# Attention and two feed-forward layers in one kernel: row sums broadcast by two reads with 64 outermost rows, the store of x on SyncE's queue, a new fixed order

## The chip, the cores and the metric

The kernel runs on one core of one Trainium2 chip. The metric is the device time in microseconds (us) of one execution; less is better. The kernel before was timed in 3 runs: a median of 1224.97 us, from 1221.14 to 1226.95.

## The reference

Causal attention over 4 batches, 8 heads, 576 tokens and 64 values a head, mixed with a retrieval from a linear memory; its result x (2304 rows of 512) goes through two feed-forward layers of 512, 2048 and 512.

```python
scores = scale * q @ k.T                       # masked above the diagonal
a = exp(scores - scores.max(-1)); a /= a.sum(-1) + 1e-09
local = a @ v
q_p = phi(q)                                   # phi(x) = where(x > 0, x, exp(x) - 1) + 1
mem_out = (q_p @ M_prev) / (q_p @ z_prev + 1e-06)
g = sigmoid(beta)                              # one value for each head
x = g * mem_out + (1 - g) * local              # rows: tokens, columns: heads
h = x @ w_in;   x = where(h >= 1, h, where(h <= -1, 0, (h + 1) ** 2 / 4)) @ w_out
h = x @ w_in2;  x = maximum(0.01 * h, h) @ w_out2
```

## The kernel before

**Attention.** The work is cut into 16 units: 4 batches of 4 pairs of heads. `attention_unit(u)` writes down the tasks of one unit, each with an engine, a length in nanoseconds, a priority, the tasks that it needs, the buffers (`Room`) that it holds, and a due time after its end (`lag`). For one unit they are: k, q and v are loaded (`load_rows`, three DMAs each, on SyncE's queue); k and q are transposed by TensorE (k1, q1) and split into a high and a low part (k2, k3, q2, q3); GpSimd sets the last 64 rows of the two heads apart (`apart`, q4); phi(q) is formed (f1 to f3). The scores come in four parts s0 to s3 (`products`, L484 and L491); VectorE adds the mask and takes the row minimum of the negated scores (L506); ScalarE takes the exponential with its sum (L510). The exponentials are transposed in five groups (`turn`, TensorE at L419, ScalarE copies at L519) into `pa` and four `pb`. The product with v goes into the PSUM buffer O in three tasks: v0 (`values_a`, L534), v1 and v2 (`values_b`, L541 to L544).

**The row sums.** n1 computes the memory's norms into O (L550). l1 to l4 (VectorE, L555 to L560) turn the 9 columns of sums and 10 columns of norms into gate divided by sum, l5 (TensorE, L561) transposes the 19 columns into 19 rows of 128, l6 (ScalarE, L563) copies them to `rt`, l7 (SyncE, L564) writes them to the DRAM tensor `r_d[u]` of 19 rows in one DMA. l8 (SyncE, `spread`, L573) reads them back in three DMAs into R, a buffer of 128 partitions (64 for each of the two heads) by 2 planes by 576: plane 0 holds the factors of the softmax, columns 0 to 511 and 512 to 575 in a read each, plane 1 those of the memory. Each read has the source shape 2 x 64 x n, in which the 64 is a broadcast: every partition of a head gets the same row.

**The end of a unit.** m1 (TensorE, L582) forms the product with the memory in a W bank of PSUM. x1 (VectorE, `weigh`, L588, two steps) multiplies O by plane 0 of R, x2 (VectorE, L591) the W bank by plane 1, x3 (GpSimd, L593) adds the two planes, and a DMA issued by GpSimd (L594) stores the result in `x_d[b]`.

**The order.** `Plan.order()` makes one fixed order for each engine from the lengths, priorities (`10 * u + PRIO[key]`), needs, buffers and due times; `STAY` is a cost for TensorE to change its kind of matmul. No engine deviates from its order at run time. `ROOMS` says how many buffers of each kind there are: one O, three W, two R, two each of q, k and v. `EARLY` = 10 of the 16 half matrices of the first layer's weights are decoded by tasks of the same plan (`weight_half`), the others by the layers' own code. The 16 units, these tasks and the first two chunks of x for the first layer (`first_chunk`, after the four stores of batch 0) share the plan.

**The layers.** Behind the plan, `layer1_steps` and `layer2` go over chunks of 256 rows. They load x from `x_d`, split each operand into a high and a low part, and use three products for one. Their order is not touched by the change.

Of the kernel before, what the change touches and what calls it, by code (L numbers as in the profile page):

```python
# [8 lines left out]
F32 = mybir.dt.float32  # L9
# [8 lines left out]
B, H, S, D = 4, 8, 576, 64  # L18
NT, DM, DFF = B * S, H * D, 2048
NP = H // 2  # L20
# [18 lines left out]

PRIO = dict(load=-48.26, v=-40.11, mem=-30.82, k=-3.3, q=-1.74, phi=35.91, s0=-19.51, s1=-15.79, s2=6.04, s3=-14.57, ta=-66.58, tb0=-44.92,  # L40
            tb1=-21.43, tb2=-29.5, tb3=-16.11, v0=-23.74, n=-32.83, l=-36.92, v1=6.21, v2=23.96, m=23.51, x=55.42, w=(2.48, 4.3, 19.15), c=1.18)
EARLY, STAY = 10, 1.25
EVACUATE = dict(ta="ACT", tb0="ACT", tb1="ACT", tb2="ACT", tb3="ACT")
# [93 lines left out]
def attn_moe_moe_kernel(ctx, tc, q, k, v, m_prev, z_prev, beta, w1i, w1o, w2i, w2o, out):  # L137
    nc = tc.nc
# [10 lines left out]
    dram = ctx.enter_context(tc.tile_pool(name="dram", bufs=1, space=bass.MemoryType.DRAM))  # L149
# [75 lines left out]
    def at(room):  # L225
        return tiles[room.kind][room.slot]


    r_d = [dram.tile([19, 128], F32, name=f"r_d{u}") for u in range(B * NP)]
    x_d = [dram.tile([DM, S], F32, name=f"x_d{b}") for b in range(B)]  # L230
# [175 lines left out]
    act, vec, pe, pool = nc.scalar, nc.vector, nc.tensor, nc.gpsimd  # L406
# [16 lines left out]
    stored, memory_of = [], {}  # L423
    SEND = 570

    def attention_unit(u):
        b, p = UNITS[u]

        def add(engine, cost, key, after, rooms, fn, mode=None, lag=None):
            return plan.add(engine, cost, 10 * u + PRIO[key], after, rooms, fn, mode, lag)  # L430

        q, k, v = Room("q"), Room("k"), Room("v")
        ks, qs, ph, st, R, O = Room("ks"), Room("qs"), Room("ph"), Room("st"), Room("R"), Room("O")
# [8 lines left out]
        if p == 0:  # L442
            memory_of[b] = mem = Room("mem")
            memory_of[b] = mem, add("SP", 2 * SEND + 2 * SEND, "mem", (), [mem], load_mem)
        mem, ld_m = memory_of[b]
# [4 lines left out]
        t = Room("W")  # L450
# [6 lines left out]
        t = Room("W")  # L457
# [4 lines left out]
        q3 = add("DVE", dve(S), "q", [q2], [t, qs], lambda t=t: vec.scalar_tensor_tensor(  # L462
            out=at(qs)[:, 1, 0:S], in0=at(t)[:, 0:S], scalar=-0.125, in1=as_r(at(qs)[:, 0, 0:S]), op0=ALU.mult, op1=ALU.subtract))
# [6 lines left out]

        q4 = add("POOL", 600, "q", [q3], [qs], apart)
        f1 = add("ACT", from_psum(S), "phi", [q1], [t, ph], lambda t=t: act.activation(at(ph)[:, 0:S], at(t)[:, 0:S], AF.Exp))
# [90 lines left out]
        l6 = add("ACT", 180, "l", [l5], [O, rt], lambda: act.activation(at(rt)[0:19], at(O)[0:19, 384:512], AF.Copy))  # L563
        l7 = add("SP", 300, "l", [l6], [rt], lambda: nc.sync.dma_start(out=r_d[u], in_=at(rt)[0:19]), lag=2.4)  # L564

        def spread():
            flat = r_d[u].rearrange("r t -> (r t)")

            def rows(c0, step, n):
                return flat[c0:c0 + 2 * step].rearrange("(h t) -> h t", h=2)[:, 0:n].unsqueeze(1).broadcast_to([2, 64, n])  # L570

            for x, c0, c1, src in ((0, 0, 512, rows(0, 512, 512)), (0, 512, S, rows(1024, 64, 64)), (1, 0, S, rows(1152, 640, S))):
                nc.sync.dma_start(out=at(R)[:, x, c0:c1], in_=src)  # L573

        l8 = add("SP", 3 * SEND, "l", [l7], [R], spread, lag=2.5)
        v1 = add("PE", 1100, "v1", [tb[0], tb[1], ld_v], [pb[0], pb[1], v, O], lambda: values_b((0, 1)), "C")
# [9 lines left out]
        def weigh():  # L586
# [6 lines left out]
        x3 = add("POOL", 1450, "x", [x1, x2], [R], lambda: pool.tensor_tensor(at(R)[:, 0], at(R)[:, 0], at(R)[:, 1], ALU.add))  # L593
        stored.append(add("POOL", 1000, "x", [x3], [R], lambda: pool.dma_start(  # L594
            out=x_d[b][128 * p:128 * p + 128], in_=at(R)[:, 0])))
# [455 lines left out]
```

## Time and profile before

| what | value |
|---|---|
| median of 3 runs | 1224.97 us (1221.14 to 1226.95) |
| the profiled execution: its time | 1222.64 us |
| its span, first to last instruction | 1220.8 us |
| busy: TensorE, VectorE, ScalarE, GpSimd | 1072.3, 769.9, 515.2, 76.9 us |
| mean granted TensorE clock | 0.911 |
| moved by DMA | 110.94 MB, mean 91 GB/s |

The rows below come from one profiled execution. PE is TensorE's matmuls, PEld its weight loads, DVE VectorE, ACT ScalarE, POOL GpSimd, SP SyncE; a q behind a name (SPq) is what the engine's sequencer does, such as issuing a DMA. Times are us from the start of the span. "L573" is a line of the kernel. In a timeline row the brackets give the idle time of the engine ahead of the instruction and what ended it. The granted clock is a share of 2.4 GHz: 1.00 is the high level, 0.50 the low one (1.2 GHz). The DMA share is the mean busy share of 16 DMA engines; by its way of counting it can pass 1.

### The profile page before, as it was taken

How to read it: one execution, taken by the hardware profiler on the slowest of the kernel's cores; microseconds unless marked ns; L12 is line 12 of the kernel's file. 1: busy time of each engine (PE TensorE's matmuls, PEld its weight loads, DVE VectorE, ACT ScalarE, POOL GpSimd, SP SyncE). 2: the span in 40 equal slices, each digit the busy share in tenths (PEclk: the TensorE clock that was granted, in tenths of full speed). 3: DMA queues.
4: the chain of work that ended last, by engine and by line, in shares of the span. 5: the costliest groups of instructions: out<-in, count | busy, mean ns of one | idle time of the engine just before them, and what ended most of it. 6: DMA issues, size and time to landing. Idle time of an engine off the chain costs nothing.

```text
span 1220.8 us, 18534 instructions
## 1 busy us (share of the span) xinstructions
PE 1072.3 (88%) x7016; PEld 944.2 (77%) x7016; DVE 769.9 (63%) x1708; ACT 515.2 (42%) x988; POOL 76.9 (6%) x105
## 2 busy tenths in 40 slices
PE   6756667776766689999999999999999999999998
PEld 5544546555655467888898878899999999999997
DVE  5545556343433266648966766689888789775665
ACT  5534445443543034334453323345444445443432
POOL 1101011001101100000000000000000000121111
PEclk9767677776786699999999999999999999999999
DMA  5432442333211133224512542422332311122121
GB/s 125 124 89 85 110 133 64 85 110 85 73 53 45 40 113 95 83 91 138 156 53 79 163 133 92 138 70 87 121 104 94 98 53 53 53 77 80 54 86 52
DMA packets 124504, 110.94 MB, mean 91 GB/s; under 512 B 70224, under 2 KB 105600, under 8 KB 124416
## 3 DMA queue, kind: packets, MB, share of 16 engines
q1 hardware_dynamic: 121648, 104.49, 28.5%
q0 software_dynamic: 1280, 4.72, 1.0%
q8 instruction: 55, 0.90, 0.3%
q10 hardware_dynamic: 1488, 0.56, 0.2%
q14 instruction: 33, 0.27, 0.1%
HBM read 86.00 MB, written 23.75 MB: 90 GB/s over the span
## 4 chain that ended last, share of the span: by engine, by line
PE 67%; DMA 21%; DVE 7%; ACT 2%; issue 2%; SPq 1%; POOL 0%; DVEq 0%; ACTq 0%
DMA R<-r_d 19%; PE A L783 5%; PE A L782 5%; PE A L781 5%; PE A L711 5%; PE A L712 5%; PE A L710 5%; PE W L419 3%; PE y L806 3%; PE y L805 2%; PE y L804 2%; PE W L491 2%; PE y L740 2%; PE y L741 2%; PE y L742 2%
## 5 line engine op out<-in xcount | busy, mean ns | idle before, releaser
L783 PE MATMUL A<-ffn_x,i 128*128 128x256 f32 x576 | 163.1, 283 | 0.0
L781 PE MATMUL A<-ffn_x,i 128*128 128x256 f32 x576 | 163.0, 283 | 0.0
L782 PE MATMUL A<-ffn_x,i 128*128 128x256 f32 x576 | 163.0, 283 | 0.0
L720 ACT ACTIVATE g<-A 128x512 f32<-128x512 f32 (+1 forms) x80 | 44.3, 554 | 217.9 <-PE A L712 215.6
L419 PE MATMUL W<-ident,e 128*128 128x128 f32 x400 | 78.6, 353 | 65.5 <-DVE R L591 57.1
L419 PEld LDWEIGHTS W<-ident,e 128*128 128x128 f32 x400 | 62.0, 186 | 78.3 <-DVE R L591 60.0
L978 ACT ACTIVATE gh<-g 128x896 fp32r<-128x896 f32 x72 | 68.8, 955 | 124.8 <-PE A L805 72.4
L722 DVE SCALAR_TENSOR_TENSOR g<-A,g 128x512 f32<-128x512 f32 (+1 forms) x80 | 50.8, 635 | 96.5 <-ACT g L721 96.4
L783 PEld LDWEIGHTS A<-ffn_x,i 128*128 128x128 f32 x576 | 110.6, 192 | 0.0
L781 PEld LDWEIGHTS A<-ffn_x,i 128*128 128x128 f32 x576 | 110.6, 192 | 0.0
L782 PEld LDWEIGHTS A<-ffn_x,i 128*128 128x128 f32 x576 | 110.6, 192 | 0.0
L957 DVE TENSOR_TENSOR gl<-g,gh 128x896 fp32r<-128x896 f32 x72 | 86.6, 1203 | 33.4 <-ACT gh L978 33.4
L519 ACT ACTIVATE pb<-W 128x640 f32<-128x640 f32 x64 | 42.9, 675 | 147.2 <-PE W L419 147.0
L506 DVE CUSTOM_DVE_ANT_0 e<-W,mask 128x128 f32<-128x128 f32 (+3 forms) x144 | 67.7, 517 | 56.5 <-PE W L491 47.4
L510 ACT ACTIVATE e<-e,mx 128x128 f32<-128x128 f32 (+3 forms) x144 | 82.5, 574 | 18.7 <-DVE mx L506 18.5
L786 ACT ACTIVATE g<-A 128x512 f32<-128x512 f32 x72 | 42.8, 594 | 88.8 <-PE A L783 86.1
L829 POOL TENSOR_TENSOR ys<-ys,pp 128x512 f32<-128x512 f32 x16 | 27.1, 1718 | 751.3 <-DVE ys L824 751.3
L591 DVE TENSOR_TENSOR R<-W,R 128x576 f32<-128x576 f32 x16 | 12.1, 757 | 94.1 <-DMA R<-r_d 94.1
L710 PE MATMUL A<-ffn_x,i 128*128 128x512 f32 (+1 forms) x160 | 59.8, 374 | 11.1 <-DVE R L591 11.1
L534 PE MATMUL O<-pa,v 128*64 128x256 f32 (+1 forms) x128 | 20.3, 457 | 48.5 <-DVE R L588 48.2
L711 PE MATMUL A<-xl,i 128*128 128x512 f32 (+1 forms) x160 | 59.0, 369 | 0.6 <-DVE xl L683 0.6
L711 PE MATMUL A<-ffn_x,i 128*128 128x512 f32 (+1 forms) x160 | 59.4, 371 | 0.0
(212 smaller groups left out, 3034.0 us busy)
## 6 DMA issues: line engine op xcount, KB each, us to landing
raw<-in_moe_w_in_dram SPq DMA_DIRECT2D x32, 512.0 KB
raw<-in_moe_w_out_dram SPq DMA_DIRECT2D x32, 512.0 KB
xf<-y_d SPq DMA_DIRECT2D x18, 512.0 KB
xf<-x_d SPq DMA_DIRECT2D x10, 512.0 KB
R<-r_d SPq DMA_DIRECT2D x16, 288.0 KB
x_d<-R POOLq DMA_DIRECT2D x16, 288.0 KB, 2.4
xf<-yp_d SPq DMA_DIRECT2D x9, 512.0 KB
op_d<-ys SPq DMA_DIRECT2D x18, 256.0 KB
```

Of the source, the lines that this page charges most:

```text
L419: pe.transpose(t[:, c:c + 128], x, ident)
L506: lambda t=t, x=x, w=w, c=512 * h + c, mk=mk, col=col: vec.tensor_tensor_reduce(out=at(x)[:, 0:w], in0=at(t)[:, c:c + w], in1=mk, op0=ALU. ...
L510: lambda x=x, w=w, col=col: act.activation(at(x)[:, 0:w], at(x)[:, 0:w], AF.Exp, bias=at(st)[1][:, col:col + 1], scale=-1.0, accum_out=at( ...
L710: nc.tensor.matmul(hx, wh, xh[:, ct], start=(ct == 0), stop=False)
L711: nc.tensor.matmul(hx, wh, xl[:, ct], start=False, stop=False)
L712: nc.tensor.matmul(hx, wl, xh[:, ct], start=False, stop=(ct == 3))
L722: nc.vector.scalar_tensor_tensor(out=g, in0=hp, scalar=1.0, in1=g, op0=ALU.max, op1=ALU.min)
L781: nc.tensor.matmul(o, wh, xh[:, ct], start=(s == 0 and ct == 0), stop=False)
L782: nc.tensor.matmul(o, wh, xl[:, ct], start=False, stop=False)
L783: nc.tensor.matmul(o, wl, xh[:, ct], start=False, stop=(s == 1 and ct == 3))
L957: nc.vector.tensor_tensor(gl, g[:, 1:8], as_r(gh), ALU.subtract)
L978: nc.scalar.activation(gg[1], gg[0][:, 1:8], AF.Copy)
```

## The change

`r_d[u]` becomes a tensor of 2 heads x 2 planes x 640. `rows_out` (l7) writes it in three DMAs instead of one: the 8 rows of columns 0 to 511 of plane 0, the 10 rows of plane 1, and the row that holds columns 512 to 575 of plane 0 for both heads. `spread` (l8) reads it in two DMAs instead of three, one for each head: the destination is 64 partitions of R with both planes, the source shape is 64 x 2 x 576 with the broadcast outermost. The store of x is issued by SyncE instead of GpSimd, as a task of the plan. The lengths and due times in the plan are changed for four tasks: `apart` from 600 to 1150 ns, l7 from 300 to 900, l8 from 1710 to 1140 with the due time from 2.5 to 2.8 us, the store from 1000 on GpSimd to 570 on SyncE. All priorities and `STAY` have new values, so each engine's fixed order in the attention part is another one.

```diff
--- before.py
+++ after.py
@@ -37,9 +37,9 @@
 FETCH = {1: [24 + 4 * i for i in range(NW)] + [47 + 3 * i // 2 for i in range(16 - NW)]}
 HALVES = {N1: [82 + 7 * i // 2 for i in range(16)], N1 + 1: [x for x in range(150, 209) if x % 8 in (0, 6)]}
 
-PRIO = dict(load=-48.26, v=-40.11, mem=-30.82, k=-3.3, q=-1.74, phi=35.91, s0=-19.51, s1=-15.79, s2=6.04, s3=-14.57, ta=-66.58, tb0=-44.92,
-            tb1=-21.43, tb2=-29.5, tb3=-16.11, v0=-23.74, n=-32.83, l=-36.92, v1=6.21, v2=23.96, m=23.51, x=55.42, w=(2.48, 4.3, 19.15), c=1.18)
-EARLY, STAY = 10, 1.25
+PRIO = dict(load=-34.99, v=-34.71, mem=-17.36, k=6.9, q=2.05, phi=36.36, s0=-38.24, s1=-31.4, s2=-4.93, s3=-16.38, ta=-63.58, tb0=-50.65,
+            tb1=-47.88, tb2=-40.64, tb3=-25.41, v0=-11.16, n=-39.61, l=-43.76, v1=-4.8, v2=22.33, m=28.28, x=11.53, w=(0.87, 4.9, 12.08), c=-19.84)
+EARLY, STAY = 10, 5.22
 EVACUATE = dict(ta="ACT", tb0="ACT", tb1="ACT", tb2="ACT", tb3="ACT")
 ROOMS = dict(W=3, O=1, q=2, k=2, v=2, mem=2, ks=2, qs=2, ph=2, st=2, R=2, rt=2, e128=4, e256=4, e384=4, e512=4, e576=2,
              pa=2, pb0=1, pb1=1, pb2=1, pb3=1)
@@ -226,7 +226,7 @@
         return tiles[room.kind][room.slot]
 
 
-    r_d = [dram.tile([19, 128], F32, name=f"r_d{u}") for u in range(B * NP)]
+    r_d = [dram.tile([2, 2, 640], F32, name=f"r_d{u}") for u in range(B * NP)]
     x_d = [dram.tile([DM, S], F32, name=f"x_d{b}") for b in range(B)]
     yp_d = [dram.tile([128, 4, TC], F32, name=f"yp_d{c}") for c in range(NCH)]
     y_d = [dram.tile([128, 4, TC], F32, name=f"y_d{c}") for c in range(NCH)]
@@ -468,7 +468,7 @@
                 r = slice(64 * h, 64 * h + 64)
                 pool.tensor_copy(x[r, :, S + 64 * h:S + 64 * h + 64], x[r, :, 512:S])
 
-        q4 = add("POOL", 600, "q", [q3], [qs], apart)
+        q4 = add("POOL", 1150, "q", [q3], [qs], apart)
         f1 = add("ACT", from_psum(S), "phi", [q1], [t, ph], lambda t=t: act.activation(at(ph)[:, 0:S], at(t)[:, 0:S], AF.Exp))
         f2 = add("DVE", 370, "phi", [f1], [ph], lambda: vec.tensor_scalar(
             out=at(ph)[:, 0:S], in0=at(ph)[:, 0:S], scalar1=1.0, scalar2=None, op0=ALU.min))
@@ -561,18 +561,18 @@
         l5 = add("PE", 110, "l", [l4], [st, O], lambda: pe.transpose(at(O)[:, 384:512], sums(), ident), "T")
         rt = Room("rt")
         l6 = add("ACT", 180, "l", [l5], [O, rt], lambda: act.activation(at(rt)[0:19], at(O)[0:19, 384:512], AF.Copy))
-        l7 = add("SP", 300, "l", [l6], [rt], lambda: nc.sync.dma_start(out=r_d[u], in_=at(rt)[0:19]), lag=2.4)
+        def rows_out():
+            x = at(rt)
+            nc.sync.dma_start(out=r_d[u][:, 0, 0:512].rearrange("h (i t) -> h i t", i=4), in_=x[0:8])
+            nc.sync.dma_start(out=r_d[u][:, 1].rearrange("h (i t) -> h i t", i=5), in_=x[9:19])
+            nc.sync.dma_start(out=r_d[u][:, 0, 512:S], in_=x[8:9])
 
         def spread():
-            flat = r_d[u].rearrange("r t -> (r t)")
-
-            def rows(c0, step, n):
-                return flat[c0:c0 + 2 * step].rearrange("(h t) -> h t", h=2)[:, 0:n].unsqueeze(1).broadcast_to([2, 64, n])
-
-            for x, c0, c1, src in ((0, 0, 512, rows(0, 512, 512)), (0, 512, S, rows(1024, 64, 64)), (1, 0, S, rows(1152, 640, S))):
-                nc.sync.dma_start(out=at(R)[:, x, c0:c1], in_=src)
-
-        l8 = add("SP", 3 * SEND, "l", [l7], [R], spread, lag=2.5)
+            for h in range(2):
+                nc.sync.dma_start(out=at(R)[64 * h:64 * h + 64], in_=r_d[u][h, :, 0:S].unsqueeze(0).broadcast_to([64, 2, S]))
+
+        l7 = add("SP", 3 * 300, "l", [l6], [rt], rows_out, lag=2.4)
+        l8 = add("SP", 2 * SEND, "l", [l7], [R], spread, lag=2.8)
         v1 = add("PE", 1100, "v1", [tb[0], tb[1], ld_v], [pb[0], pb[1], v, O], lambda: values_b((0, 1)), "C")
         v2 = add("PE", 1000, "v2", [v1, tb[2], tb[3]], [pb[2], pb[3], v, O], lambda: values_b((2, 3, 4)), "C")
         m = Room("W")
@@ -591,7 +591,7 @@
         x2 = add("DVE", dve(S), "x", [m1, l8], [m, R], lambda: vec.tensor_tensor(
             at(R)[:, 1], at(m)[:, 0:S], at(R)[:, 1], ALU.mult))
         x3 = add("POOL", 1450, "x", [x1, x2], [R], lambda: pool.tensor_tensor(at(R)[:, 0], at(R)[:, 0], at(R)[:, 1], ALU.add))
-        stored.append(add("POOL", 1000, "x", [x3], [R], lambda: pool.dma_start(
+        stored.append(add("SP", SEND, "x", [x3], [R], lambda: nc.sync.dma_start(
             out=x_d[b][128 * p:128 * p + 128], in_=at(R)[:, 0])))
 
     def weight_half(n, f, x):
```

## Rows read from the trace of the kernel before

**Rows 1.** The page, part 4: shares of the chain, by engine, then by line.

```profile
PE 67%; DMA 21%; DVE 7%; ACT 2%; issue 2%; SPq 1%; POOL 0%; DVEq 0%; ACTq 0%
DMA R<-r_d 19%; PE A L783 5%; PE A L782 5%; PE A L781 5%; PE A L711 5%; PE A L712 5%; PE A L710 5%; PE W L419 3%; PE y L806 3%; PE y L805 2%; PE y L804 2%; PE W L491 2%; PE y L740 2%; PE y L741 2%; PE y L742 2%
```

**Rows 2.** Stretches (from:to): length, busy PE, PEld, DVE, ACT, POOL, clock, DMA share, GB/s.

```profile
0.00:423.00 423.00, 289.19 (x1880) 224.71 (x1880) 186.35 (x540) 186.48 (x459) 46.24 (x85) 0.75 0.32 87
860.00:1010.00 150.00, 150.00 (x1253) 150.00 (x1252) 121.36 (x269) 67.45 (x94) 0.00 (x0) 1.00 0.28 92
```

**Rows 3.** The chain in order of time: start us, length us, what.

```profile
29.24 15.79 DMA R<-r_d
...
114.73 9.56 DMA R<-r_d
...
264.38 15.23 DMA R<-r_d
```

**Rows 4.** Timeline of one unit: start, us, engine, line, operation [idle before, releaser].

```profile
238.04 0.26 SPq L564 DMA_DIRECT2D r_d<-rt  x1
...
239.77 4.35 SPq L573 DMA_DIRECT2D R<-r_d  x3
...
244.22 6.07 SPq L388 DMA_DIRECT2D k<-in_k_dram  x2
...
247.74 0.42 DVE L588 TENSOR_TENSOR R<-O,R 128x256 f32<-128x256 f32 x1 [0.18 <-DMA R<-r_d]
...
250.14 0.87 PE L534 MATMUL O<-pa,v 128*64 128x256 f32 x8 [1.66 <-DVE R L588]
...
256.06 0.76 DVE L591 TENSOR_TENSOR R<-W,R 128x576 f32<-128x576 f32 x1 [5.30 <-DMA R<-r_d]
...
256.87 2.18 PE L419 MATMUL W<-ident,e 128*128 128x128 f32 x9 [4.15 <-DVE R L591]
```

**Rows 5.** Stretches of one microsecond: a read of R alone; loads in flight.

```profile
418.00:419.00 1.00, 0.00 (x0) 0.00 (x0) 0.00 (x0) 0.00 (x0) 0.00 (x0) 0.50 0.13 51
260.00:261.00 1.00, 1.00 (x8) 0.78 (x7) 0.33 (x3) 0.00 (x0) 0.00 (x0) 0.50 1.10 397
```

**Rows 6.** Timeline: norms, loads on SyncE's queue, the add on GpSimd.

```profile
251.55 1.18 PE L550 MATMUL O<-zz,ph 128*128 128x2 f32 x10
...
255.80 1.09 SPq L388 DMA_DIRECT2D q<-in_q_dram  x2
...
256.95 1.49 POOL L593 TENSOR_TENSOR R<-R 128x576 f32<-128x576 f32 x1 [5.51 <-issue]
```

**Rows 7.** Stretches: high clock, low clock, one whole period.

```profile
24.00:34.00 10.00, 9.55 (x83) 7.25 (x84) 6.85 (x23) 8.88 (x26) 0.00 (x0) 1.00 0.33 90
257.00:266.00 9.00, 9.00 (x46) 6.93 (x46) 4.48 (x19) 5.38 (x17) 2.01 (x2) 0.50 0.64 190
280.00:303.00 23.00, 17.88 (x116) 13.66 (x116) 8.85 (x29) 10.86 (x27) 2.62 (x4) 0.72 0.28 78
```

**Rows 8.** The page, part 6: the store of x, KB, median us to landing.

```profile
x_d<-R POOLq DMA_DIRECT2D x16, 288.0 KB, 2.4
```

**Rows 9.** Timeline of TensorE: an unbroken run at the high clock.

```profile
51.40 1.61 PE L491 MATMUL W<-ks,qs 64*128 64x128 f32 x18
...
57.03 0.77 PE L419 MATMUL W<-ident,q 128*128 128x128 f32 x5
...
57.63 1.19 PE L582 MATMUL W<-ph,mz 128*128 128x512 f32 x4
...
59.90 0.77 PE L419 MATMUL W<-ident,e 128*128 128x128 f32 x5
```

**Rows 10.** Timeline: first reads on SyncE, first and last L591 on VectorE.

```profile
28.08 3.78 SPq L573 DMA_DIRECT2D R<-r_d  x3
...
45.12 0.76 DVE L591 TENSOR_TENSOR R<-W,R 128x576 f32<-128x576 f32 x1 [5.24 <-DMA R<-r_d]
...
422.59 0.76 DVE L591 TENSOR_TENSOR R<-W,R 128x576 f32<-128x576 f32 x1 [5.52 <-DMA R<-r_d]
```


## The prediction

> **What bounds the kernel now.** I read the chain of work that ended last first. TensorE carries 67% of it, a DMA 21%, and nearly all of that DMA share is one transfer, the broadcast of the row sums into R (19% of the span of 1220.8 us, some 230 us) [rows 1]. The split by stage comes next: attention runs up to about 423 us at a mean granted clock of 0.75, with TensorE busy 289 of 423 us, VectorE and ScalarE about 186 each; behind it the feed-forward part is TensorE work without gaps (150.00 of 150 us in the stretch shown, clock 1.00) [rows 2]. So nothing in the second part can be bought by this change, and all there is to win lies in the first 423 us.
>
> What rules the first part is seen in the chain in order of time: it holds 16 pieces "R<-r_d", one for each unit, two of them about 10 us long and the others 14.5 to 15.8 us; from the ninth unit on one comes some 23 us after the other [rows 3]. One unit followed in the timeline shows how they pace everything [rows 4]. The sums are written to DRAM (L564) at 238.04; they have landed when L573 begins at 239.77, 1.73 us later; the three reads of L573 follow. VectorE has the first part at 247.74 (L588) and the last at 256.06 (L591), 16.3 us after the first read was issued. TensorE waits 1.66 us for the O buffer behind L588 (the values at L534) and 4.15 us for a W bank behind L591 (the transposes at L419).
>
> Why are the reads slow? Where a read of R is alone, the DMA engines are busy 0.13 of 16, that is two engines, at 51 GB/s; in another microsecond, with loads of 128 rows in flight, the sixteen moved 397 GB/s [rows 5]. The three reads have an outermost dimension of 2. The loads on SyncE's queue suffer with them: two k loads behind the reads hold the queue for 6.07 us [rows 4], where two q loads with no read just ahead of them take 1.09 [rows 6].
>
> There is a second loss. The granted clock is 0.50 (1.2 GHz) from 257 to 266 us, behind the 4 us in which TensorE stood still. At this level 46 matmuls fill 9 us; in a stretch at 1.00 (2.4 GHz) 83 need 9.55 [rows 7]. So each unit pays for the stall and then again for the clock.
>
> **The reads.** The bytes stay: 256 + 32 + 288 KB before, 2 x 288 after. If 64 outermost rows are taken by all sixteen engines, as the loads of 128 are, 576 KB take 1.5 us at 397 GB/s instead of 11.6 us at 51. The fixed part is about what the 9.5 KB of the sums need from issue to landing, 1.73 us [rows 4]. With two issues at 0.55 us (half of 1.09 [rows 6]) that is 1.1 + 1.7 + 1.5 = 4.3 us from first issue to last landing; I take 4.5, against 16.3 now. The lower bound is 3 us (the 288 KB store of x, all 128 rows at once, lands in 2.4 us [rows 8], and the second read is issued 0.55 later); the upper is 16.3 us, if sixteen engines get no more out of two rows than two do.
>
> One detail counts against the change: now L588 needs only the first two reads, and O is given back at 250.1, 10.3 us after the first issue [rows 4]. Afterwards each read carries both planes for 64 partitions, so L588 needs both. O is then released 4.5 + 0.9 us after the first issue: O gains some 5 us where the W bank gains 12.
>
> The Trainium skill speaks against halves: DMA: Bandwidth & Descriptors, section "Rules for kernel authors", says that two transfers to disjoint halves of the partitions aren't worth it, since both run on the same engines one behind the other. By that rule the second read would land a whole transfer later, up to 1.9 us for each unit (2.4 less the 0.55 by which it is issued later anyway) and 28 us over 15 units if nothing hid it; the total would be 1094 in place of 1066. The row of two engines at 0.13 says that the gain is in the number of engines and not in the halves.
>
> **The sums on their way out.** One write of 19 rows becomes three. An issue of L564 takes 0.26 us [rows 4]; two more with 0.1 us between them put 0.7 us ahead of the landing. The landing itself stays, I take it, at 1.73 us: the bytes are few, and no row shows such a small write on more or fewer engines (bounds 1.2 and 2.7, a microsecond below and above at most). From written out to landed reads: 2.4 + 4.5 = 6.9 us in place of 18.0.
>
> **x on SyncE's queue.** It leaves GpSimd's queue, which is busy 46 of 423 us [rows 2], so nothing is won there. On SyncE it costs one issue of 0.55 to 0.6 us, and the queue now stands still until GpSimd's add of unit u is done: the add begins 0.9 us behind L591's start and takes 1.49 [rows 4, 6]. Queued behind the store are later loads (k, v, q, raw) and the write of unit u+1's sums. That write can't be ready sooner: it needs O of unit u+1, which L588 of unit u gives back, and then values, norms, reciprocals and the transpose of the sums, some 4 us in all, so a store placed between them waits in a gap. Loads that come late have a second buffer. I take 0, and keep 1 us for each unit as the upper bound. SyncE's issues for one unit: 9 loads x 0.55, a raw and a quarter of the memory loads 1.2, writes 1.1, reads 1.1, store 0.6 = 9 us, which fits in a unit of 15.
>
> **The new order.** The trace of before doesn't show it; what can be read are floors that no order passes. TensorE at the high level: from 51.40 to 59.90 us an unbroken run holds all scores, both parts of the values on pb, the transposes for pa and for q, and the memory product, 8.50 us; q alone is 57.63 - 57.03 = 0.60 [rows 9]. Left of a unit are k (0.60), the transposes for three pb with five blocks like q (1.80) and one with four (0.50), the first values 0.8 [rows 4], the norms 1.1 [rows 6] and the transpose of the sums 0.2: together 13.5 us. VectorE and ScalarE: 186/16 = 11.7 us for one unit [rows 2]. The chain through the one O buffer: first values 0.9, norms 1.2, small VectorE steps and the transpose of the sums 1.4, rt 0.3, out and back 6.9, L588 0.95 = 11.7 us. TensorE is next in line, with three others close behind it, in queues that run in order; to its 13.5 I add 15%, 15.5 us for one unit. From 24 to 34 us, with nothing to wait for from R, TensorE was busy 9.55 of 10 us [rows 7]; but the weights' decoding sits unevenly on VectorE, and where it does VectorE is the longer one. I expect the clock to stay at 1.00 for most of the stage, as it did from 24 to 34 us, where pauses were short.
>
> **The sum.** L591 of the first unit starts at 45.12, of the last at 422.59: 15 periods of 25.2 us [rows 10]. After: the first reads are issued at 28.1, as now, and have landed by 32.6; L591 follows the two steps of L588 at 33.5. Then 15 x 15.5 = 232.5: the last at 266. What follows is the same work as now behind 422.6. So 422.6 - 266 = 156.6 us come off the 1222.64 us of the profiled execution: 1066. (That execution lies 2.3 us under the median of the runs shown and within their spread.)
>
> **Rivals.**
> TensorE at its floor (0.08): 15 x 13.5 = 202.5, last L591 at 236, 1036 us. For it: gaps under 5% from 24 to 34 us. Against: three other limits within 2 us.
> Half of the gain (0.20): a wait on SyncE (in order, now with the store's wait in it) or the decoding on VectorE makes TensorE pause in many units, and the clock falls as it does now. At the low level 46 matmuls in 9 us make 22.7 us for the 116 of a unit [rows 7]; with half of each unit at it the period is 18 us: 33.5 + 270 = 303.5, 1104 us. At the low level throughout: 33.5 + 340 = 373.5, 1174 us.
> The reads scale in part (0.05): they land after 9 us in place of 4.5; the O chain is 16.2 us and the period about 18, again 1104.
> The reads don't scale (0.04), the case that ends slower: all engines fetch from the same two rows of sums, and the trace never shows more than two engines there. If the rate stays at 51 GB/s, the landing stays at 16 us, and each unit pays 0.7 us for the writes and 0.6 us for the store's issue on the queue on which the chain runs: 16 x 1.3 = 21, 1243 us. It decides once the reads land as late as now. Against it: each of the two engines now moves 25 GB/s there, as much as each of sixteen does for loads (397/16), so the rows aren't what holds two engines back.
> Nothing to see (0.01): between these two.
> My forecast, a period of 14 to 17 us, 1043 to 1088: 0.62.
>
> **Chances and range.** A measurement tells some 0.5%, 6 us, from no change. Faster 0.95, same 0.01, slower 0.04. The range reaches from TensorE's floor to a period of 19 us (33.5 + 285 = 318.5, 1118.5), say 1036 to 1120.
>
> **What would show it.** Right: the pieces "R<-r_d" leave the chain or shrink below 6 us; the DMA share while they run is near 1; from L573 to L591 some 5 us; L591 every 15 to 16 us; a granted clock above 0.9 up to 266 us; loads behind the reads no longer hold SyncE. Wrong: L591 later than 8 us behind L573 (reads don't scale); clock 0.50 inside units, with TensorE waiting for VectorE or for loads (half of the gain); the write of the sums waiting behind the store of x; weights of the first layer not decoded when attention ends, so that the feed-forward part begins with a hole.

## The result and the profile after

The changed kernel takes 1081.58 us (median of 4 runs, 1076.08 to 1084.03) against 1223.34 us (the three runs of the kernel before that are given above, and a fourth): 0.883 of the time before, 95% interval 0.879 to 0.887. The forecast was 1066, with a range from 1036 to 1120. The profiled execution took 1081.57 us; its parts are these (the page's span, its row of granted clock in 40 slices, and the shares of the chain by engine and by line; compare [rows 1]):

```profile
span 1079.8 us, 18564 instructions
...
PEclk9998897999899999999999999999999999999999
...
PE 65%; DVE 6%; ACT 2%; issue 1%; DVEq 0%; ACTq 0%
...
PE A L783 6%; PE A L782 6%; PE A L781 6%; PE A L711 6%; PE A L710 5%; PE A L712 5%; PE y L806 3%; PE y L805 3%; PE y L804 3%; PE y L740 2%; PE y L741 2%; PE y L742 2%; PE A L741 2%; PE A L742 2%; PE A L740 2%; PE h L804 1%
```

These shares add up to 74%: the chain on this page begins at the last L591 and says nothing of attention.

```profile
276.27 0.68 DVE R L591
```

So it doesn't show whether the read of the sums, 19% of the chain before, has left the chain. In the trace of the kernel with the W banks moved (below), where the chain goes back to the start, the read still has 5% of it (4.7%, some 50 us), in pieces of 4.3 to 6.9 us in place of 9.6 to 15.8. Three of them:

```profile
161.21 6.91 DMA R<-r_d
...
211.83 4.67 DMA R<-r_d
...
225.96 4.31 DMA R<-r_d
```

The stretches (columns as in [rows 2]; the whole attention part, two stretches of 4 us inside it, and the rest) show attention itself:

```profile
0.00:276.00 276.00, 236.49 (x1856) 183.92 (x1856) 183.44 (x539) 182.17 (x456) 35.56 (x70) 0.93 0.59 134
...
100.00:104.00 4.00, 4.00 (x26) 3.80 (x22) 3.61 (x8) 2.77 (x4) 1.99 (x3) 0.58 0.70 119
...
172.00:176.00 4.00, 4.00 (x24) 3.85 (x20) 0.62 (x1) 1.41 (x2) 1.41 (x1) 0.54 0.85 246
...
276.00:1079.00 803.00, 788.75 (x5160) 724.37 (x5160) 583.32 (x1170) 330.49 (x532) 30.08 (x19) 1.00 0.29 92
```

Attention now lasts 276 us in place of 423, for nearly the same busy time of VectorE and ScalarE (183 and 182 us); TensorE is busy 236 us in place of 289, because the mean granted clock rose from 0.75 to 0.93. It isn't 1.00: between 100 and 190 us there are stretches at 0.5 to 0.6. The second part lasts 5.4 us longer than before (see the W banks below).

One unit in the timeline, the counterpart of [rows 4] and [rows 6]:

```profile
238.13 0.63 SPq L566 DMA_DIRECT2D r_d<-rt  x1
...
241.11 1.27 SPq L572 DMA_DIRECT2D R<-r_d  x2
...
244.94 0.92 SPq L388 DMA_DIRECT2D v<-in_v_dram  x2
...
246.31 0.82 DVE L588 TENSOR_TENSOR R<-O,R 128x256 f32<-128x256 f32 x2
...
247.05 0.75 DVE L591 TENSOR_TENSOR R<-W,R 128x576 f32<-128x576 f32 x1
...
247.19 0.87 PE L534 MATMUL O<-pa,v 128*64 128x256 f32 x8 [0.42 <-DVE R L588]
```

The first write of the sums is issued at 238.13, the first read at 241.11, and L588 begins at 246.31, 5.2 us after the reads' issue in place of 8.0 for its first step and 9.8 for its second before. L591 follows at once, where it began 16.3 us after the issue. TensorE's matmuls wait 0.42 us for O and nothing for a W bank. The v loads behind the reads are issued in 0.92 us; before, two k loads there took 6.07 [rows 4]. First and last L591 on VectorE [rows 10]:

```profile
34.98 0.75 DVE L591 TENSOR_TENSOR R<-W,R 128x576 f32<-128x576 f32 x1
...
276.19 0.75 DVE L591 TENSOR_TENSOR R<-W,R 128x576 f32<-128x576 f32 x1
```

241.2 us for 15 periods: 16.1 us each, before 25.2.

### The profile page after: what moved, and what is told of

It reads as the page before. It is cut to its first block, busy times and chain, and to the rows that moved or that the text cites. A ratio compares the mean times of both kernels' runs of the same rounds, so it can differ in the third digit from the quotient of the medians.

```text
span 1079.8 us, 18564 instructions
## 1 busy us (share of the span) xinstructions
PE 1025.2 (95%) x7016; PEld 908.3 (84%) x7016; DVE 766.8 (71%) x1708; ACT 512.7 (47%) x988; POOL 65.6 (6%) x89
## 4 chain that ended last, share of the span: by engine, by line
PE 65%; DVE 6%; ACT 2%; issue 1%; DVEq 0%; ACTq 0%
PE A L783 6%; PE A L782 6%; PE A L781 6%; PE A L711 6%; PE A L710 5%; PE A L712 5%; PE y L806 3%; PE y L805 3%; PE y L804 3%; PE y L740 2%; PE y L741 2%; PE y L742 2%; PE A L741 2%; PE A L742 2%; PE A L740 2%; PE h L804 1%
## 5 line engine op out<-in xcount | busy, mean ns | idle before, releaser
L506 DVE CUSTOM_DVE_ANT_0 e<-W,mask 128x128 f32<-128x128 f32 (+2 forms) x144 | 66.8, 517 | 39.9 <-PE W L491 35.2
L510 ACT ACTIVATE e<-e,mx 128x128 f32<-128x128 f32 (+2 forms) x144 | 82.5, 574 | 13.7 <-DVE mx L506 13.5
L710 PE MATMUL A<-ffn_x,i 128*128 128x512 f32 (+1 forms) x160 | 60.0, 375 | 9.1 <-DVE R L591 9.1
L419 PE MATMUL W<-ident,e 128*128 128x128 f32 x400 | 63.0, 304 | 2.5 <-ACT pb L519 1.3
L787 DVE TENSOR_TENSOR g<-g 128x128 f32<-128x128 f32 x72 | 29.5, 410 | 46.4 <-ACT g L786 46.4
L711 PE MATMUL A<-ffn_x,i 128*128 128x512 f32 (+1 forms) x160 | 59.6, 373 | 0.0
L712 PE MATMUL A<-ffn_x,i 128*128 128x512 f32 (+1 forms) x160 | 59.6, 372 | 0.0
L419 PEld LDWEIGHTS W<-ident,e 128*128 128x128 f32 x400 | 50.6, 159 | 10.2 <-issue 2.8
```

Of the source, the lines that this page charges most:

```text
L419: pe.transpose(t[:, c:c + 128], x, ident)
L506: lambda t=t, x=x, w=w, c=512 * h + c, mk=mk, col=col: vec.tensor_tensor_reduce(out=at(x)[:, 0:w], in0=at(t)[:, c:c + w], in1=mk, op0=ALU. ...
L510: lambda x=x, w=w, col=col: act.activation(at(x)[:, 0:w], at(x)[:, 0:w], AF.Exp, bias=at(st)[1][:, col:col + 1], scale=-1.0, accum_out=at( ...
L710: nc.tensor.matmul(hx, wh, xh[:, ct], start=(ct == 0), stop=False)
L711: nc.tensor.matmul(hx, wh, xl[:, ct], start=False, stop=False)
L712: nc.tensor.matmul(hx, wl, xh[:, ct], start=False, stop=(ct == 3))
```

## The experiments

All times are medians of whole executions. The table takes from each trace the starts of L591. Units are counted from 0; "middle" is the time for units 5 to 9, "late" the mean period of units 10 to 14, "rest" from the last L591 to the end of the span.

| kernel | median us | ratio to before | last L591 | middle | late | rest |
|---|---|---|---|---|---|---|
| changed kernel | 1081.58 | 0.883 (0.879 to 0.887) | 276.2 | 91.0 | 14.0 | 803.6 |
| reads only, old order | 1087.20 | 0.888 (0.886 to 0.890) | 287.1 | 84.0 | 15.2 | 798.2 |
| old reads, new order | 1237.20 | 1.011 (1.008 to 1.014) | 431.1 | | | 803.4 |
| store on GpSimd | 1078.51 | 0.882 (0.879 to 0.884) | 273.9 | 85.1 | 14.0 | 803.5 |
| W banks moved | 1074.31 | 0.878 (0.876 to 0.880) | 273.7 | 90.0 | 14.0 | 797.8 |
| raw loads behind the reads | 1080.26 | 0.885 (0.879 to 0.890) | 276.4 | 88.6 | 14.0 | 803.6 |
| 62 and 2 rows | 1274.28 | 1.043 (1.040 to 1.045) | 469.2 | | | 804.0 |
| half the bytes | 1064.45 (1 run) | | 259.1 | 81.0 | 13.7 | 803.6 |
| different rows | 1070.19 (1 run) | | 264.7 | 83.3 | 13.7 | 803.7 |
| W banks moved, store on GpSimd | 1076.98 | 0.879 (0.874 to 0.885) | 276.6 | 88.2 | 13.9 | 798.3 |
| W banks moved, two writes on ScalarE | 1063.74 | 0.869 (0.865 to 0.872) | 263.7 | 81.8 | 13.7 | 797.9 |
| W banks moved, memory product repeated | 1077.51 | 0.880 (0.876 to 0.883) | 279.8 | 83.4 | 14.4 | 797.8 |

**The reads alone.** The kernel before with the new layout, writes and reads; the planner's lengths stay, and with them every engine's order.

```diff
-    r_d = [dram.tile([19, 128], F32, name=f"r_d{u}") for u in range(B * NP)]
+    r_d = [dram.tile([2, 2, 640], F32, name=f"r_d{u}") for u in range(B * NP)]
...
+        l7 = add("SP", 300, "l", [l6], [rt], rows_out, lag=2.4)
```

> The kernel before with the new layout of the sums, the three writes and the two reads, and nothing else: old priorities and lengths, so each engine keeps its old order, and x is stored by GpSimd. If the reads carry the gain (my theory): the pieces of 15 us go, L591 comes every 16 to 17 us, 1075 to 1100 us. If the new order carries a good part (rival): the old order, made for other lengths, stalls TensorE elsewhere and the time stays above 1120 us.

1087.2 us: 136 of the 142 us come from the reads (with their three writes). The new order and the store together give the other 6: by the two traces 11 in attention (last L591 at 276.2 in place of 287.1), of which 5.4 are lost behind it (rest).

**The old reads in the new order.** The changed kernel with the one write of 19 rows and the three reads with an outermost dimension of 2.

```diff
-            for h in range(2):
-                nc.sync.dma_start(out=at(R)[64 * h:64 * h + 64], in_=r_d[u][h, :, 0:S].unsqueeze(0).broadcast_to([64, 2, S]))
...
+            for x, c0, c1, src in ((0, 0, 512, rows(0, 512, 512)), (0, 512, S, rows(1024, 64, 64)), (1, 0, S, rows(1152, 640, S))):
+                nc.sync.dma_start(out=at(R)[:, x, c0:c1], in_=src)
```

> The changed kernel with the old write of 19 rows and the old three reads with an outermost dimension of 2, in the new order and with the store of x on SyncE. If the reads carry the gain: 25 us for one unit again, 1215 to 1250 us (the store of x on SyncE now waits in a queue that is held, which may add some). If the new order helps by itself: under 1190 us.

1237.2 us, 1.1% slower than before. Without fast reads the new order with the store on SyncE is worth nothing, and loses 13 us.

**62 and 2 rows.** The same bytes in four reads, and still many rows outermost.

```diff
-                nc.sync.dma_start(out=at(R)[64 * h:64 * h + 64], in_=r_d[u][h, :, 0:S].unsqueeze(0).broadcast_to([64, 2, S]))
+                for c, n in ((0, 62), (62, 2)):
+                    nc.sync.dma_start(out=at(R)[64 * h + c:64 * h + c + n], in_=r_d[u][h, :, 0:S].unsqueeze(0).broadcast_to([n, 2, S]))
```

> The changed kernel with each read of 64 rows split into one of 62 rows and one of 2 rows; the bytes are the same, and 62 rows are still outermost. If the number of engines is one that divides the outermost rows (62 = 2 x 31, so 2): the DMA share falls to 0.13 again, landing 14 us or more after the first issue, 1190 to 1240 us. Rival, it is enough that many rows are outermost: two more issues, landing 6.5 to 7 us, 1085 to 1105 us.

1274.3 us, slower than the kernel before. Timeline of one unit, and one microsecond in which a read was alone (columns as in [rows 5]):

```profile
369.39 5.26 SPq L573 DMA_DIRECT2D R<-r_d  x4
...
375.10 3.67 SPq L388 DMA_DIRECT2D v<-in_v_dram  x2
...
385.49 0.82 DVE L589 TENSOR_TENSOR R<-O,R 128x256 f32<-128x256 f32 x2 [9.05 <-DMA R<-r_d]
```

```profile
407.00:408.00 1.00, 0.00 (x0) 0.00 (x0) 0.00 (x0) 0.00 (x0) 0.00 (x0) 0.50 0.13 51
```

The share is 0.13 at 51 GB/s, two engines again; L588 comes 16.1 us after the first issue, and two v loads behind the reads hold the queue for 3.67 us. The time lies 34 us above the range that was expected for this case: here each read carries both planes, so L588 waits 16.1 us where before it had its first part after 8.0; that this makes up the whole difference is not tested. So it isn't the number of outermost rows that counts but what divides it: 64 rows go to all sixteen engines, 62 = 2 x 31 to two. The Trainium skill states just this (DMA: Bandwidth & Descriptors, section "Why a DMA increments its semaphore by 16 and not by 1"): the largest number up to 16 that divides the slowest dimension of both sides. The share of 0.13 agrees.

**Half the bytes, and different rows.** From the third unit on only plane 0 is read (plane 1 keeps old values, which is not what the reference computes).

```diff
+            n = 2 if u < 2 else 1
             for h in range(2):
-                nc.sync.dma_start(out=at(R)[64 * h:64 * h + 64], in_=r_d[u][h, :, 0:S].unsqueeze(0).broadcast_to([64, 2, S]))
+                nc.sync.dma_start(out=at(R)[64 * h:64 * h + 64, 0:n], in_=r_d[u][h, 0:n, 0:S].unsqueeze(0).broadcast_to([64, n, S]))
```

> The changed kernel in which from the third unit on the reads fetch plane 0 only (288 KB in place of 576); plane 1 of R then keeps what the units before left there, so this part of the computation is not the reference's. Of the 5.4 us from the reads' issue to L588 I had put 1.5 on the bytes; with the last unit's bytes seen moving for 3.2 us. If the bytes cost 3.2: landing falls to 3.7 to 4.1 us. If they cost 1.5 and the fixed part is larger: 4.6 to 4.8 us. In both cases the period of the late units falls only from 13.8 to about 13.5 us, TensorE's floor, if that floor holds.

In the other kernel the reads take 64 different rows of q of the same shape (the factors are then wrong, and the reads don't wait for the writes).

```diff
+            src = q_in[b, 2 * p:2 * p + 2].rearrange("h s d -> (h s d)").rearrange("(r x t) -> r x t", r=64, x=2)
             for h in range(2):
-                nc.sync.dma_start(out=at(R)[64 * h:64 * h + 64], in_=r_d[u][h, :, 0:S].unsqueeze(0).broadcast_to([64, 2, S]))
+                nc.sync.dma_start(out=at(R)[64 * h:64 * h + 64], in_=src)
```

> The changed kernel in which the two reads of the sums fetch 64 different rows of q, of the same shape and size (64 x 2 x 576), in place of one row 64 times; x is then not the reference's, and the reads do not wait for the landing of the sums. If sixteen engines lose time because they fetch the same 4.6 KB (the part of my rival that the reads scale in part): the bytes move in 1.5 to 2 us in place of 3.2, and L588 comes 3.7 to 4.3 us after the issue. If the rate is that of such rows on sixteen engines anyway: again about 3.2 us and 5.2 to 5.6.

The last unit's reads are the cleanest, since no load is near them. In the changed kernel they are issued at 269.96, and L588 begins at 275.45, 5.5 us later. Their bytes move in this stretch, and in the kernel with different rows in the one below it (length, busy times, clock, share, GB/s):

```profile
271.00:274.20 3.20, 0.00 (x0) 0.00 (x0) 0.00 (x0) 0.00 (x0) 0.00 (x0) 0.54 0.81 182
```

```profile
260.10:262.80 2.70, 0.00 (x0) 0.00 (x0) 0.00 (x0) 0.00 (x0) 0.00 (x0) 0.50 0.81 218
```

Timelines of the last unit with half the bytes, and with different rows:

```profile
254.71 1.14 SPq L573 DMA_DIRECT2D R<-r_d  x2
...
258.31 0.82 DVE L589 TENSOR_TENSOR R<-O,R 128x256 f32<-128x256 f32 x2 [9.38 <-DMA R<-r_d]
```

```profile
259.09 1.16 SPq L573 DMA_DIRECT2D R<-in_q_dram  x2
...
263.95 0.82 DVE L589 TENSOR_TENSOR R<-O,R 128x256 f32<-128x256 f32 x2 [9.62 <-DMA R<-in_q_dram]
```

Half the bytes: 3.6 us from issue to L588, 1.9 less than 5.5. So 576 KB cost some 3.2 to 3.8 us and not 1.5. Different rows: 4.9 us, 0.6 less and between the two cases that were expected; the bytes move in 2.7 us at 218 GB/s in place of 3.2 us at 182. But that is one pair of transfers in one trace each. In the other kernels whose reads are those of the changed kernel, the last L588 came 5.1 to 5.7 us after the issue. The shortest, with the W banks moved:

```profile
267.87 1.27 SPq L573 DMA_DIRECT2D R<-r_d  x2
...
272.97 0.82 DVE L589 TENSOR_TENSOR R<-O,R 128x256 f32<-128x256 f32 x2 [10.81 <-DMA R<-r_d]
```

Beside it the different rows are only 0.2 us ahead, and unlike the sums they had not been written just before. So what it costs that sixteen engines fetch one row many times is not shown; it is small beside the 16.1 us of two engines. Different rows don't reach 397 GB/s either, so the microsecond of [rows 5] was no measure for this transfer. The 182 and 218 are means that take in how the transfer starts and ends; its best microsecond is faster:

```profile
272.00:273.00 1.00, 0.00 (x0) 0.00 (x0) 0.00 (x0) 0.00 (x0) 0.00 (x0) 0.50 1.09 300
```

How much of the gap belongs to the shape of the reads and how much to their shortness is not tested. In both kernels the late units stay at 13.7 us although the sums come back sooner: there the reads are not the bound, and TensorE's floor of 13.5 us is near. The middle units get 8 to 10 us shorter.

**Raw loads behind the reads.** In four units a 512 KB load is issued just ahead of the reads. Timeline of unit 5 in the changed kernel:

```profile
111.11 0.38 SPq L286 DMA_DIRECT2D raw<-in_moe_w_in_dram  x1
...
112.13 1.27 SPq L572 DMA_DIRECT2D R<-r_d  x2
...
119.42 0.82 DVE L588 TENSOR_TENSOR R<-O,R 128x256 f32<-128x256 f32 x2 [2.36 <-DMA k<-in_k_dram]
...
120.29 0.87 PE L534 MATMUL O<-pa,v 128*64 128x256 f32 x8 [4.04 <-DVE R L588]
```

L588 begins 7.3 us after the reads' issue, and TensorE has waited for it (the 4.04 in brackets).

```diff
-        for t in plan.order():
+        tasks = plan.order()
+        for write, read in zip(writes, reads):
+            i, j = tasks.index(write), tasks.index(read)
+            late = [t for t in tasks[i:j] if t in raws]
...
+            tasks[i:j + 1] = [t for t in tasks[i:j + 1] if t not in late] + late
+        for t in tasks:
```

> The changed kernel with every load of raw weights that stands between the write of the sums and the reads on SyncE's queue moved right behind the reads; nothing else in the order is changed. In the changed kernel four units with such a 512 KB load issued 1 us ahead of the reads (58.8, 90.6, 112.1, 163.1 us) had VectorE's L588 7.1 to 7.9 us after the reads' issue, the others mostly 5.2 to 5.7. If the bytes ahead in the rings are the cause: all units at 5.2 to 5.8, 4 x 2 = 8 us less and a little for the clock, 1066 to 1075 us. Rival, the engines are shared whatever the order, or the later weights hold VectorE: no change, 1078 to 1085 us.

In three of the four units (58.8, 90.6 and 112.1 us) L588 came 5.5 to 6.0 us after the issue in place of 7.2 to 8.0, so the bytes ahead do delay the reads. The fourth was not cured (a raw load still stood ahead of it), and unit 0's L588 now came 9.5 us after the issue, with three raw loads issued right behind the reads. In all 1080.3 us: no gain that the runs can tell. That the raw loads are what makes the middle units slow is not shown.

**The way out of the sums.** Two of the three writes issued by ScalarE (on top of the W banks moved, below).

```diff
-            nc.sync.dma_start(out=r_d[u][:, 1].rearrange("h (i t) -> h i t", i=5), in_=x[9:19])
-            nc.sync.dma_start(out=r_d[u][:, 0, 512:S], in_=x[8:9])
+            act.dma_start(out=r_d[u][:, 1].rearrange("h (i t) -> h i t", i=5), in_=x[9:19])
+            act.dma_start(out=r_d[u][:, 0, 512:S], in_=x[8:9])
```

> The kernel with the W buffers in other banks, and the second and third write of the sums issued by ScalarE, which has just made them, in place of SyncE. On SyncE three writes took 3.07 us from the first issue to the reads (223.95 to 227.02), where one write took 1.73. If the way out of the sums holds up the slow units (from 80 to 190 us): 1.2 us less for each of some 9 units, 1062 to 1069 us; the late units stay at 13.8 us, TensorE's floor. Rival, the two issues delay ScalarE's exponentials by as much: 1072 to 1080 us.

```profile
240.51 0.63 SPq L567 DMA_DIRECT2D r_d<-rt  x1
...
240.51 0.57 ACTq L568 DMA_DIRECT2D r_d<-rt  x1
...
241.13 0.58 ACTq L569 DMA_DIRECT2D r_d<-rt  x1
...
242.94 1.25 SPq L573 DMA_DIRECT2D R<-r_d  x2
...
248.41 0.82 DVE L589 TENSOR_TENSOR R<-O,R 128x256 f32<-128x256 f32 x2 [0.28 <-DMA R<-r_d]
```

From first write to first read 2.43 us in place of 2.98 in the unit shown above, a gain of 0.5 us for each unit where 1.2 were expected. 1063.7 us, 10.6 less than with the banks alone, the fastest kernel of this study, 0.869 of before. The middle units give 8.2 us of it and the late ones, already at TensorE's floor, 0.3 each. So the shorter way out of the sums makes the middle units shorter, by more than the 0.5 us a unit that it saves itself. In this pair of traces 7.4 of the 8.2 us lie in units 8 and 9, and 5.6 of them in unit 9, in which the granted clock fell with the banks alone and stayed at 1.00 here. The same stretch in both, the banks alone first:

```profile
168.00:188.00 20.00, 18.82 (x110) 14.56 (x111) 8.25 (x28) 9.48 (x25) 1.98 (x3) 0.66 0.42 109
```

```profile
168.00:188.00 20.00, 19.72 (x171) 15.65 (x172) 12.66 (x44) 13.81 (x37) 3.15 (x4) 1.00 0.52 137
```

With the banks alone TensorE had waited 3.07 us for O at 166.1 to 169.2, just ahead of the low stretch. Units 5 and 6 took the same 37.2 us in both. What SyncE gains by issuing two writes less is not told apart from the shorter way.

**The W banks.** In the changed kernel the first matmul of the feed-forward part waits, and ScalarE's first step on it starts 6 us after the last L591:

```profile
276.99 0.80 PE L710 MATMUL A<-ffn_x,i 128*128 128x512 f32 x1 [9.10 <-DVE R L591]
```

```profile
282.18 0.60 ACT L720 ACTIVATE g<-A 128x512 f32<-128x512 f32 x1 [15.21 <-PE A L712]
```

In the order before, the last unit's memory product lay in the second W buffer, in the new one it lies in the first. The buffers are moved:

```diff
+    tiles["W"] = [tiles["W"][i] for i in (2, 0, 1)]
```

> The changed kernel with the three W buffers in other PSUM banks: the one that holds the last unit's memory product is moved from the first two banks to the fifth and sixth. In the changed kernel the first layer's first matmuls (L710) stand still for 9.1 us until L591 gives the first banks back, where in the kernel before two steps had run before such a wait. If the 5.3 us that the second part became longer come from this: L710 starts right after the last memory product, from the last L591 to the end 5 to 7 us less, 1074 to 1077 us. Rival, the second part is longer for another reason (weights decoded later): L710 moves and the end doesn't, 1080 to 1083 us.

The same ScalarE step, and TensorE's wait for L591, which now comes after the first matmuls (list of waits: who waited for whom, us in total, times, longest us):

```profile
268.69 0.60 ACT L721 ACTIVATE g<-A 128x512 f32<-128x512 f32 x1 [3.81 <-PE A L713]
```

```profile
PE A L711 <- DVE R L592: 5.9, 1, 5.9
```

ScalarE's step is at 268.69, ahead of the last L591 at 273.7, and the rest falls from 803.6 to 797.8 us: 5.8 less in the trace, 7.3 in the median. The 5.4 us that the second part had become longer lie in the choice of that buffer. The column "rest" agrees: 803.4 to 804.0 us in the kernels with the new order and the banks unmoved, the one with the old reads among them, 797.8 to 798.3 in those with the banks moved, 798.2 with the old order.

**The store.** The changed kernel with the store issued by GpSimd, then the same with the W banks moved.

```diff
-        stored.append(add("SP", SEND, "x", [x3], [R], lambda: nc.sync.dma_start(
+        stored.append(add("SP", SEND, "x", [x3], [R], lambda: pool.dma_start(
```

> The changed kernel with the store of x issued by GpSimd again, at the same place of the fixed order. By my prediction (the store on SyncE costs nothing): within 4 us of the changed kernel, 1078 to 1086 us. Rival, SyncE's wait for GpSimd's add holds up the next unit's write of the sums or its loads: 1060 to 1072 us, with the stretches from 100 to 190 us shorter.

> The kernel with the W buffers in other banks, and the store of x issued by GpSimd again. The changed kernel with that store alone measured 1078.51 beside 1081.58 us, which is inside what the runs scatter. If the store on SyncE costs nothing, as predicted: 1071 to 1077 us, as with the banks alone (1074.31). If it holds up SyncE: 1066 to 1071 us.

3.1 us less without the other edit and 2.7 us more with it: two differences of opposite sign, each within what the runs scatter. No cost and no gain of the store's queue can be told. SyncE's longest sums of waits in the changed kernel up to 280 us (us, times, longest):

```profile
SPq L566 <- ACT pb L519: 18.9, 8, 3.6
...
SPq L594 <- POOL R L593: 16.0, 8, 3.2
...
SPq L572 <- DMA r_d<-rt: 12.8, 24, 1.2
```

The store waits 16 us in all for GpSimd's add. The write of the sums (L566) waits longer, and for ScalarE: 18.9 us in the row shown, 44 us with its other rows of the same list.

**TensorE kept at work.** The low clock in the middle units began where TensorE waited for O. The memory product of units 4, 5 and 8 is computed three times, with the same result, ahead of that wait.

```diff
-            for c0, c1 in ((0, 512), (512, S)):
+            for c0, c1 in ((0, 512), (512, S)) * (3 if u in (4, 5, 8) else 1):
```

> The kernel with the W buffers in other banks, in which the memory product of the units 4, 5 and 8 is computed three times in a row instead of once, 2.3 us more work for TensorE each, at the place where it otherwise waits 1.4 to 4 us for O. It is there that the granted clock fell to 0.50, for 7 to 15 us each time. If the waits of TensorE bring the clock down and that costs the middle units their time: the clock stays at 1.00 over most of 95 to 190 us, these periods fall from 18 to 19 us to 15 to 16, 1064 to 1071 us in all. Rival, the low clock is only a sign of a chain that is late anyway: clock near 1, the same time, 1072 to 1078 us, or more by the added work.

The stretch from 98 to 188 us, with the banks alone and with the repeated product:

```profile
98.00:188.00 90.00, 80.22 (x579) 62.31 (x580) 60.52 (x170) 58.96 (x145) 11.21 (x17) 0.85 0.60 137
```

```profile
98.00:188.00 90.00, 83.37 (x650) 62.96 (x649) 65.39 (x182) 63.74 (x159) 11.37 (x17) 0.96 0.70 155
```

The clock is 0.96 in place of 0.85, 650 matmuls fit in (24 of them the repeats) where there were 579, and the five middle units take 83.4 us in place of 90.0. But the whole execution isn't shorter (1077.5 against 1074.3): in this profiled execution the units 0 to 4 took longer by about 9 us, most of it ahead of the first repeated product, and the clock still fell in two places, near 190 us and here:

```profile
140.00:152.00 12.00, 11.55 (x76) 9.37 (x77) 9.36 (x26) 6.56 (x19) 2.66 (x3) 0.72 0.32 66
```

So in this pair of traces the repeated work went with a higher clock in the units that got it; the whole time is the one that was expected of the rival, and that the repeats pay is not shown.

## Why the prediction was right, and where 15.6 us went

The predicted 1066 and the profiled 1081.57 differ by 15.6 us: 1.5 at the first L591 (34.98 in place of 33.5), 15 x 0.58 = 8.7 in the periods (16.08 in place of 15.5), and 5.4 behind the last L591.

**What bounds the kernel** held: the reads with an outermost dimension of 2 were the cause, since the change of the reads (with their writes) alone gives 136 of 142 us, and without it nothing is gained. The rival that the reads don't scale fell. The loss by the clock was read rightly too: TensorE's busy time in attention fell by 53 us for nearly the same matmuls (1880 up to 423 us before, 24 of them of the first layer, 1856 after).

**The reads** were mis-sized. Forecast 4.5 us, measured 5.2 to 5.5 without a load near them, 7.2 to 8.0 behind a raw load. The term that failed is the bytes: 1.5 us at 397 GB/s, where 3.2 us at 182 GB/s were measured. I took the rate from a microsecond of other transfers, and left out the start and end of this one. The rival "the reads scale in part" was thus true in kind: from 51 to 182 GB/s, not to 397; but the landing stayed under its 9 us. The fixed part, 1.7 us and 1.1 for two issues, was about right (5.5 - 3.2 = 2.3). By the Trainium skill's rule on halves (DMA: Bandwidth & Descriptors, section "Rules for kernel authors") the prediction's working would have given 1094. That time did not come. But the trace doesn't show the two landings apart, only that the bytes of both halves moved in one stretch of 3.2 us, and no run reads all 128 partitions in one DMA on sixteen engines; so what the second half costs is not shown.

**The sums on their way out**: 2.4 us forecast, 2.96 to 3.14 measured in thirteen of the sixteen units (5.4 and 4.2 in the first two, 3.4 in another). The landing term held (1.65 us after the last issue at 239.46). The issues didn't: I took the 0.26 us of the one write of 19 rows for each of them, and in the unit shown they take 0.57 to 0.63.

**x on SyncE's queue**: taken at 0, and no cost could be told.

**The new order**: TensorE's floor of 13.5 us was met, in the units without weights, as 13.8 to 14.2; with shorter landings they stay near it (13.7 on average), so something close to it is a floor. The first layer's weights cost what I had lumped into "15%": they stand in units 0 to 9, where a unit takes 18.2 us in the middle five. There the chain through O is the bound: TensorE waits 1.1 to 4.0 us for O in each of these units, and half the bytes or a shorter way out make them shorter. It was forecast at 11.7 us, with no step waiting for another in its engine's queue. On the way to the sums of unit 5 their transpose came 9 us after the first values, at a clock of 0.62 and behind other work of TensorE. That the mean of all units still came within 0.6 us of the 15.5 is in part luck: the middle units ran slower than that and the late ones faster. The rival "half of the gain" described these units rightly (a period near 18, the clock falling behind TensorE's waits), for about a third of them; that SyncE's wait for the store is its cause was not borne out (no cost could be told), and VectorE's decoding was not tested by itself.

**What follows is the same work** is the step that was wrong in kind, by 5.4 us: the work is the same, but where it can begin depends on which PSUM banks the last unit's buffers leave free. I had the wait in the trace of before, where TensorE stopped at 412 us after two steps of the first layer, and didn't ask what the new order would make of it:

```profile
411.89 0.39 PE L712 MATMUL A<-ffn_x,i 128*128 128x512 f32 x1
423.40 0.80 PE L710 MATMUL A<-ffn_x,i 128*128 128x512 f32 x1 [11.12 <-DVE R L591]
```

The prediction did name a hole at the start of the feed-forward part as a sign of being wrong, but for another reason, weights that are not decoded.

## What to carry to other kernels

Look at the DMA share of a slow transfer alone: 0.13 of sixteen engines is two, and the dimension that stands outermost, on either side, says why; 64 rows freed it, 62 would not have. Take the rate of a new transfer, and the cost of its issue, from one of its own shape and size. When a planner reassigns buffers, check which of them the next stage needs first.

## What the runs showed of the hardware

Reads that use two engines (DMA share 0.13) hold SyncE's queue: in the units shown, two loads behind them took 6.07 and 3.67 us to issue, against 0.92 behind the new reads and 1.09 with no read just ahead. A DMA of 19 rows of 128 took 0.26 us to issue, each of the three writes that replace it mostly 0.56 to 0.67; which property of their shapes makes the difference was not tested. Reading one row 64 times moved 576 KB in 3.2 us (182 GB/s), reading 64 rows in 2.7 us (218 GB/s), and from issue to L588 the first took 5.1 to 5.7 us in the traces of several kernels, the second 4.9 in its one trace. In 98 to 188 us, 2.3 us more work ahead of three waits went with a mean granted clock of 0.96 in place of 0.85.
